# Four mixed layers on one core: six more tiles turned by way of DRAM, sums in another order, weight pieces bunched

## The chip, the cores and the metric

The kernel runs on one core of a Trainium2 chip. The metric is device time in microseconds (us) of one execution, as the median of several runs; before the change it is 1407.29 us (3 runs, 1407.14 to 1407.45). The core has five engines with a queue of instructions each: TensorE (PE in the profile, with PEld for its weight loads), VectorE (DVE), ScalarE (ACT), GpSimd (POOL) and SyncE (SP), which in this kernel issues all DMAs.

## The reference

Two kinds of layer take turns, A, B, A, B, each added to `x` (2048 rows of 512, float32), with the same weights in both rounds. Cut to what matters:

```python
def _A_ref(x, wqkv, wo):
    B, S, D = x.shape
    H = 32; Dh = D // H
    qkv = (lambda x, *d: x.transpose(*d))((x @ wqkv).reshape(B, S, 3, H, Dh), 2, 0, 3, 1, 4)
    q, k, v = qkv[0], qkv[1], qkv[2]
    phi = lambda t: jnp.where(t > 0, t + 1, jnp.exp(t)) + 1e-6
    pq, pk = phi(q), phi(k)
    kv = jnp.einsum("bhsd,bhse->bhde", pk, v)
    z = jnp.einsum("bhsd->bhd", pk)
    num = jnp.einsum("bhqd,bhde->bhqe", pq, kv)
    den = jnp.einsum("bhqd,bhd->bhq", pq, z)[..., None] + 1e-6
    o = num / den
    return (lambda x, *d: x.transpose(*d))(o, 0, 2, 1, 3).reshape(B, S, D) @ wo

def _B_ref(x, w_in, w_sp, b_sp, w_out):
    z = _gelu(jnp.einsum("bsd,df->bsf", x, w_in))
    z1 = z[..., :Fh]
    z2 = _layernorm(z[..., Fh:], axis=-1)
    g = jnp.einsum("ts,bsf->btf", w_sp, z2) + b_sp[None, :, None]
    return jnp.einsum("bsf,fd->bsd", z1 * g, w_out)

x = x + _A_ref(_layernorm(x, axis=-1), A_wqkv, A_wo)
x = x + _B_ref(_layernorm(x, axis=-1), B_w_in, B_w_sp, B_b_sp, B_w_out)
```

and the last two lines once more.

## The kernel before

The rows are cut into 16 tiles of 128 (`NT`). Every product is done as three matmuls (`mm3`, L133 to L135): each operand is split into a high half, a copy to fp32r on ACT (`high`, L119), and a low half, what is left, on DVE (`low`, L122); high by high, high by low and low by high are added up in PSUM. The order of instructions is written out by hand (`manual_schedule`): each engine runs its queue in the order in which the program names them, and waits where an operand or a buffer isn't ready.

`P1` is the first half of layer kind A, run once for each of the two rounds (`L` is 0 or 1; the text calls them first and second layer). `P1.run` has 17 steps `s`. In a step the kernel loads the rows of tile s+3, takes the statistics of tile s+2 on DVE (`ln_a`, L196 and L198) with three small operations on POOL (L200 to L203), normalises that tile on ACT (`ln_b`, L209), turns tile s (`T_high`, `T_low`), multiplies tile s-1 with the k weight (`K`) and, up to step 10, with the q weight (`Q`), applies phi to both (`phi`: L327 and L328 on ACT, L329 on DVE), splits the normalised rows (`xsplit`) and phi of k (`K_split`: L340 on ACT, L341 on DVE) and adds phi of k to the running sum on POOL (L346). `Gmm` then multiplies tile s-2's rows with its phi of k into four PSUM banks. So PE has 36 matmuls of 128x512 in a step with Q, 24 in one without. The q products of the last six tiles (`DEFER`, `later`) are done one by one afterwards, in `transition` and the first steps of `P2` (`late`, `late_phi`).

A tile is turned in one of two ways (`Turn`). By PE: the normalised tile is kept, four transposes of 128x128 go to a bank (L221), and ACT and DVE split it from there. By DRAM: ACT writes the normalised rows in another order of features, SP stores them to `xt` (L245), loads them back a step later (L249 by way of L115), and one DVE instruction (L260) turns blocks of 32x32 into a page, from which ACT and DVE split. `P1` turns tiles 10 to 15 by PE in both layers, and in the first layer tiles 0 to 2 as well; the others go by DRAM.

Beside its tiles, a step of `P1.run` also splits one piece of the weights that come next (`side`: 4 pieces of v, 4 of the output weight, 7 of `win2`; `Weight.piece` is one ACT and one DVE instruction, `fetch` one DMA). And in the first layer POOL makes sums of blocks of `w_sp` for the products of `P4`, two adds a tick (`Sums.tick`, L788), with the sums of the tick before stored to DRAM and three or one new blocks loaded; 32 ticks in all, in steps 2 to 7 of `P1`, from step 8 of `P2`, and in `P4`. In `P1` these blocks lie in two of the four large buffers `bg`.

`transition` leads from `P1` to `P2` (the rest of layer kind A and the input product of B). The first tiles of `P2` are prepared there: `a` multiplies on POOL (L567), `a2_den` takes sums and reciprocals on DVE (L579 to L581), `a2_mul` scales on DVE (L588) and copies on ACT (L240). Steps 1 to 4 of `P2.run` turn tile s by PE: `c` is the product of tile s-1, `c2` adds it to `x` (L620) and takes the statistics, `b_low` makes the low half of tile s (L122). `P4` does the product with `w_sp` and the gating; while its last loop runs over the 16 output tiles, `join` starts the next `P1`: loads, tiles 0 and 1, and the k and q weights, fetched at i = 8 and 10 and split one piece of each at i = 10 to 13.

SBUF is dealt out in slots by hand (22 pages of 128x512, 6 `qd`, 4 `bg`, and 8 PSUM banks), each list first in, first out; an instruction that fills a slot waits for the last reader of what was in it.

Of the kernel before, what the change touches and what calls it, by code (L numbers as in the profile page):

```python
# [13 lines left out]
OP = mybir.AluOpType  # L14
# [5 lines left out]
NT = S // P  # L20
# [6 lines left out]
DEFER = 6  # L27
# [44 lines left out]
def mixer_kernel(ctx: ExitStack, tc: tile.TileContext, x_in, wqkv, wo_d, win1_d, win2_d, wsp_d, bsp_d, wout_d,  # L72
                 ident_d, mask_d, out_d):
    nc = tc.nc
# [7 lines left out]
    pages = Slots(main, "pg", 22)  # L82
    quads = Slots(main, "qd", 6)
    bigs = Slots(main, "bg", 4)
# [180 lines left out]
    class P1:  # L265
        def __init__(self, L):
            self.L = L
            self.st = 2 * L
            self.x, self.ms, self.xT, self.pk, self.kb, self.r, self.xhl = {}, {}, {}, {}, {}, {}, {}
            self.wk, self.wq, self.wv = (w_square(wqkv, 512), w_square(wqkv, 0, True), w_square(wqkv, 1024))  # L270
            self.wo, self.win2 = w_wo(), w_in2()
            self.later = deque(range(NT - DEFER, NT))
            self.turn = Turn(f"xt{L}", (*((0, 1, 2) if L == 0 else ()), *range(NT - DEFER, NT)))
            self.G = None
            self.zacc = None

# [60 lines left out]
        def K_split(self, i):  # L337
            r = self.r.pop(i)
            h, l = pages.get(PAGE, F32R), pages.get(PAGE, F32R)
            nc.scalar.activation(h, r, AF.Copy, bias=PHI_EPS)  # L340
            nc.vector.scalar_tensor_tensor(l, r, PHI_EPS, h.bitcast(F32), op0=OP.add, op1=OP.subtract)  # L341
            self.pk[i] = (h, l)
            if i == 0:
                self.zacc = r
            else:
                nc.gpsimd.tensor_tensor(self.zacc, self.zacc, r, op=OP.add)  # L346
                pages.put(r)

        def Q(self, i):
            self.qb = self.proj(i, self.wq)  # L350
# [78 lines left out]
        def run(self, sums):  # L429
            side = deque()  # L430
            for w in (self.wv, self.wo, self.win2):
                side.extend([w] * len(w.pieces))
            side[0].fetch()
            ND = NT - DEFER
            for s in range(1, NT + 2):
                self.loadx(s + 3)
                self.turn.load(s + 1)
                if 2 <= s < NT:
                    self.T_high(s)
                if s == 1:  # L440
                    if not self.kb:
                        self.K(0)
                    self.K(1)
                elif 2 < s <= NT:
                    self.K(s - 1)
                self.ln_a(s + 2)
                if 2 <= s < NT:
                    self.T_low(s)
                if s <= NT:
                    self.K_phi(s - 1)  # L450
                if s <= ND:
                    self.Q(s - 1)
                if s == NT + 1:
                    self.late()
                if s <= NT:
                    self.xsplit(s - 1)
                    self.K_split(s - 1)
                self.ln_b(s + 2)
                if s <= ND:
                    self.Q_phi(s - 1)  # L460
                if s >= 2:
                    self.Gmm(s - 2)
                if s == NT + 1:
                    self.late_phi()
                if self.L == 0 and s == 2:
                    sums.slots = Sheets(bigs, 2)
                if self.L == 0 and 2 <= s < 8:
                    sums.tick(s < 7)
                if self.L == 0 and s == 8:
                    sums.store()  # L470
                    sums.slots.close()
                    sums.slots = pages
                if side:
                    side.popleft().piece()
                if side:
                    side[0].fetch()
            while side:
                side.popleft().piece()


    def transition(p1, p2):
# [9 lines left out]
        for c in range(4):  # L491
# [15 lines left out]
                                op=OP.add)  # L507
# [4 lines left out]
        for q in range(4):  # L512
            b = banks.get([P, P])
            s = slice(q * P, (q + 1) * P)
# [26 lines left out]
        p2.a2_mul(1)  # L541
        p1.late()
        p2.a(3)
        p2.a2(2)
        p1.late_phi()


    class P2:
# [69 lines left out]
        def c2(self, i):  # L618
            x = self.x[i]
            nc.vector.tensor_add(x, x, self.cb)  # L620
            banks.put(self.cb)
            self.ms[i] = stats(x, 1)

        def c3(self, i):
            x = self.x.pop(i)
# [75 lines left out]
        def run(self, sums):  # L701
            w1 = self.win1
            for s in range(1, NT + 3):
                self.loadx(s + 1)
                self.qturn.load(s + 1)
                if s in self.qturn.by_pe:
                    self.c(s - 1)
                    self.b_high(s)
                    self.c2(s - 1)
                    self.b_low(s)  # L710
                    if s >= 2:
                        self.d_high(s - 2)
                        self.d_low(s - 2)
                    self.p1.late()
                    self.c3(s - 1)
                    self.a2(s + 2)
                    self.p1.late_phi()
                    self.a(s + 3)
                else:
                    if s < NT:  # L720
                        self.b_high(s)
                    self.a2_den(s + 2)
                    if s < NT:
                        self.b_low(s)
                    if s <= NT:
                        self.c(s - 1)
                        self.c2(s - 1)
                    if s == NT:
                        quads.put(*self.W2)
                        pages.put(self.zbc)  # L730
                    self.a2_mul(s + 2)
                    late = s - 2 in self.xturn.by_pe
                    if late:
                        self.d_high(s - 2)
                        self.d_low(s - 2)
                    if s <= NT:
                        self.c3(s - 1)
                    self.a(s + 3)
                    if s <= NT + 1 and not late:
                        self.d_high(s - 2)  # L740
                        self.d_low(s - 2)
                if s >= 4:
                    self.e4(s - 4)
                self.xturn.load(s - 1)
                if s >= 3:
                    self.e(s - 3)
                    self.e2(s - 3)
                    self.e3(s - 3)
                self.f()
                self.f()  # L750
                self.fq.extend(self.fnext)
                self.fnext = []
                w1.piece(True)
                w1.fetch()
                if s > 7:
                    sums.tick()
                if s >= NT + 1:
                    self.p4.fetch(s - NT - 1)
            self.e4(NT - 1)
            self.win2.free()  # L760
# [51 lines left out]
    class P4:  # L812
# [243 lines left out]
        def join(self, i, nxt):  # L1056
# [9 lines left out]
            if i in (11, 12):  # L1066
                nxt.turn.load(i - 11)
            if 10 <= i < 14:
                nxt.wk.piece()
                nxt.wq.piece()  # L1070
            if i == 14:
                nxt.T(0)
            if i == 15:
# [2 lines left out]
    sums = Sums()  # L1076
    p1 = P1(0)
    p1.start()
    for L in range(2):
        p1.run(sums)  # L1080
        p2 = P2(p1)
# [39 lines left out]
```

## Time and profile before

| | before |
|---|---|
| median of 3 runs | 1407.29 us |
| the profiled execution, its time | 1407.07 us |
| its span, first to last instruction | 1405.3 us |
| granted TensorE clock | 1.00 |
| PE busy | 1394.3 us, 99% |
| DVE busy | 889.5 us, 63% |
| ACT busy | 572.7 us, 41% |
| POOL busy | 405.8 us, 29% |
| DMA | 219.39 MB, mean 156 GB/s |

A row of a timeline has the start in us from the span's beginning, the duration, engine, line, operation, out<-in by the program's names and shapes; in brackets stands how long the engine was idle before and what ended that. A row of the view of waits reads: who waited, for whom, us in total, how often, the longest. The first layer's `P1` runs to about 132 us in the span, the second's from about 707 to 827.

### The profile page before, as it was taken

To read this page: it belongs to the slowest core of one execution; us is meant where nothing else is said; L and a number is where in the kernel's file an instruction comes from. 1 tells how busy PE (TensorE), PEld (TensorE's weight loads), DVE (VectorE), ACT (ScalarE), POOL (GpSimd) and SP (SyncE) were. 2 spreads that over 40 slices of the span, in tenths; PEclk is the share of its full clock that TensorE was granted. 3 is DMA by queue.
4 is the path that set the end of the run, shared out by engine and by line. 5 is a ranking of instruction groups with operands and counts; after the bars stand their busy time and mean duration, and the time that the engine had idled before them with its cause. 6 is when DMAs were issued, how large, how long until landed. Compare 5 with 4: busy or idle time off the path is not lost.

```text
span 1405.3 us, 17490 instructions
## 1 busy us (share of the span) xinstructions
PE 1394.3 (99%) x6318; PEld 1167.0 (83%) x6318; DVE 889.5 (63%) x1263; ACT 572.7 (41%) x871; POOL 405.8 (29%) x490
## 2 busy tenths in 40 slices
PE   9999999999999999999999999999999999999998
PEld 7788888888888888888888888888888888888887
DVE  7876786753587666583578767766415466666632
ACT  5665544434322332351366655444333233333420
POOL 3843244544366002040023334432100030022300
PEclk9999999999999999999999999999999999999999
DMA  5831156766887433443644212555335344434432
GB/s 198 258 117 46 56 177 213 258 226 204 326 299 265 133 121 136 167 163 120 210 127 142 61 38 93 183 177 163 114 119 158 105 165 134 130 120 169 152 112 90
DMA packets 134390, 219.39 MB, mean 156 GB/s; under 512 B 11552, under 2 KB 44064, under 8 KB 134304
## 3 DMA queue, kind: packets, MB, share of 16 engines
q1 hardware_dynamic: 134304, 218.28, 47.5%
q8 instruction: 49, 0.80, 0.2%
q14 instruction: 37, 0.30, 0.1%
HBM read 153.49 MB, written 64.75 MB: 155 GB/s over the span
## 4 chain that ended last, share of the span: by engine, by line
PE 93%; DVE 2%; ACT 1%; DMA 1%; POOL 1%; issue 1%; SPq 0%; ACTq 0%; DVEq 0%; POOLq 0%
PE bank L135 18%; PE bank L134 18%; PE bank L133 18%; PE bank L908 13%; PE bank L910 13%; PE bank L909 13%; PE bank L221 1%; DMA pg<-in_wqkv_dram 1%; DVE qd L122 0%; DMA pg<-in_x_dram 0%; DVE st L196 0%; DVE pg L588 0%; ACT z_q L328 0%; ACT pg L209 0%; ACT z_q L327 0%
## 5 line engine op out<-in xcount | busy, mean ns | idle before, releaser
L908 PE MATMUL bank<-qd,pg 128*128 128x512 f32 x800 | 311.3, 389 | 0.0
L910 PE MATMUL bank<-qd,pg 128*128 128x512 f32 x800 | 311.2, 389 | 0.0
L909 PE MATMUL bank<-qd,pg 128*128 128x512 f32 x800 | 311.2, 389 | 0.0
L847 DVE TENSOR_TENSOR qd<-qd,qd 128x1024 fp32r<-128x1024 f32 x112 | 151.9, 1356 | 175.6 <-ACT qd L846 175.4
L846 ACT ACTIVATE qd<-qd 128x1024 fp32r<-128x1024 f32 x112 | 118.5, 1058 | 215.8 <-PE bank L910 195.5
L935 POOL TENSOR_TENSOR bg<-bg,pg 128x512 f32<-128x512 f32 x56 | 85.5, 1562 | 408.8 <-DVE bg L962 195.5
L910 PEld LDWEIGHTS bank<-qd,pg 128*128 128x128 f32 x800 | 150.2, 188 | 31.3
L908 PEld LDWEIGHTS bank<-qd,pg 128*128 128x128 f32 x800 | 150.1, 188 | 31.3 <-DVE bg L953 0.2
L909 PEld LDWEIGHTS bank<-qd,pg 128*128 128x128 f32 x800 | 150.2, 188 | 31.2
L135 PE MATMUL bank<-qd,pg 128*128 128x512 f32 x384 | 150.7, 392 | 3.0 <-DVE pg L122 3.0
L200 POOL TENSOR_SCALAR rs<-mv 128x1 f32<-128x1 f32 x96 | 33.1, 344 | 378.8 <-DVE mv L198 378.3
L209 ACT ACTIVATE pg<-pg,nb,rs 128x512 f32<-128x512 f32 x63 | 51.0, 810 | 181.2 <-POOL nb L203 181.2
L133 PE MATMUL bank<-qd,pg 128*128 128x512 f32 x288 | 112.7, 391 | 1.4 <-ACT pg L119 1.4
L134 PE MATMUL bank<-qd,pg 128*128 128x512 f32 x288 | 112.3, 390 | 0.0
L133 PE MATMUL bank<-bg,qd 128*128 128x448 f32 x256 | 94.0, 367 | 0.0
L134 PE MATMUL bank<-bg,qd 128*128 128x448 f32 x256 | 93.6, 366 | 0.0
L135 PE MATMUL bank<-bg,qd 128*128 128x448 f32 x256 | 93.4, 365 | 0.0
L788 POOL TENSOR_TENSOR pg<-pg,pg 128x512 f32<-128x512 f32 x52 | 78.0, 1499 | 47.3 <-DMA pg<-in_wsp_dram 33.8
L135 PEld LDWEIGHTS bank<-qd,pg 128*128 128x128 f32 x384 | 72.1, 188 | 21.2 <-DVE pg L122 6.4
L135 PE MATMUL bank<-qd,bg 128*128 128x512 f32 x224 | 87.5, 390 | 0.0
L135 PE MATMUL bank<-wo,qd 128*128 128x512 f32 x224 | 87.3, 390 | 0.2 <-DVE qd L122 0.2
L134 PE MATMUL bank<-qd,bg 128*128 128x512 f32 x224 | 87.4, 390 | 0.0
(128 smaller groups left out, 2640.2 us busy)
## 6 DMA issues: line engine op xcount, KB each, us to landing
qd<-s SPq DMA_DIRECT2D x64, 512.0 KB, 3.3
qd<-in_wsp_dram SPq DMA_DIRECT2D x48, 512.0 KB, 4.0
pg<-x SPq DMA_DIRECT2D x64, 256.0 KB, 3.0
z<-pg SPq DMA_DIRECT2D x56, 256.0 KB, 2.3
pg<-z SPq DMA_DIRECT2D x56, 256.0 KB, 5.3
pg<-in_wsp_dram SPq DMA_DIRECT2D x52, 256.0 KB, 4.8
s<-pg SPq DMA_DIRECT2D x52, 256.0 KB, 4.5
x<-pg SPq DMA_DIRECT2D x48, 256.0 KB, 2.6
```

Source lines behind the costliest of these rows:

```text
L133: nc.tensor.matmul(out, ah, bh, start=start, stop=False)
L134: nc.tensor.matmul(out, ah, bl, start=False, stop=False)
L135: nc.tensor.matmul(out, al, bh, start=False, stop=stop)
L200: nc.gpsimd.tensor_scalar(rs, mv[:, 1:2], LN_EPS, None, op0=OP.add)
L209: nc.scalar.activation(y, x, AF.Identity, bias=nb, scale=rs)
L788: nc.gpsimd.tensor_tensor(t, a, b, op=OP.add)
L846: nc.scalar.activation(w[:, 0], r, AF.Copy)
L847: nc.vector.tensor_sub(w[:, 1], r, w[:, 0].bitcast(F32))
L908: m(out, h[:, o], w[:, 0, j, :], start=start, stop=False, skip_group_check=True)
L909: m(out, h[:, o], w[:, 1, j, :], start=False, stop=False, skip_group_check=True)
L910: m(out, l[:, o], w[:, 0, j, :], start=False, stop=stop, skip_group_check=True)
L935: nc.gpsimd.tensor_tensor(u, u, z1, op=OP.mult)
```

## The change

Six things are changed.

1. `P1` turns all tiles by DRAM but tiles 0 to 2 of the first layer. Tile 2 of that layer is turned at the end of step 1, no longer in step 2.
2. The running sum of phi of k is written to the page of the new summand, and the page of the old sum is given back; before it was added in place.
3. The first blocks of `w_sp` are fetched in step 1. The ticks of `P1` are in steps 2 to 5, behind the statistics and before `K_split`, no longer at the end of steps 2 to 7; those of `P2` start at step 6 instead of 8.
4. The weight pieces of `side` are split one a step up to step 5 and two a step in steps 6 to 10, and none after; they are fetched one or two ahead.
5. In the steps 1 to 4 of `P2` the statistics of tile s-1 come behind `b_low`; in `transition` the second half of `a2(2)` comes behind `late_phi`.
6. In `join` both k pieces come at i = 10 and 11 and both q pieces at i = 12 and 13.

```diff
@@ -270,7 +270,7 @@
             self.later = deque(range(NT - DEFER, NT))
-            self.turn = Turn(f"xt{L}", (*((0, 1, 2) if L == 0 else ()), *range(NT - DEFER, NT)))
+            self.turn = Turn(f"xt{L}", range(3) if L == 0 else ())
@@ -343,8 +343,9 @@
             else:
-                nc.gpsimd.tensor_tensor(self.zacc, self.zacc, r, op=OP.add)
-                pages.put(r)
+                nc.gpsimd.tensor_tensor(r, self.zacc, r, op=OP.add)
+                pages.put(self.zacc)
+                self.zacc = r
@@ -435,7 +436,8 @@
                 self.turn.load(s + 1)
-                if 2 <= s < NT:
+                turned = 2 <= s < NT and s not in self.turn.by_pe
+                if turned:
                     self.T_high(s)
@@ -444,7 +446,12 @@
                 self.ln_a(s + 2)
-                if 2 <= s < NT:
+                if self.L == 0 and s == 1:
+                    sums.slots = Sheets(bigs, 2)
+                    sums.fetch()
+                if self.L == 0 and 2 <= s < 6:
+                    sums.tick(s < 5)
+                if turned:
                     self.T_low(s)
@@ -455,6 +462,8 @@
                     self.K_split(s - 1)
+                if s + 1 < NT and s + 1 in self.turn.by_pe:
+                    self.T(s + 1)
                 self.ln_b(s + 2)
@@ -462,20 +471,14 @@
-                if self.L == 0 and s == 2:
-                    sums.slots = Sheets(bigs, 2)
-                if self.L == 0 and 2 <= s < 8:
-                    sums.tick(s < 7)
-                if self.L == 0 and s == 8:
+                if self.L == 0 and s == 6:
                     sums.store()
                     sums.slots.close()
                     sums.slots = pages
-                if side:
+                for _ in range(min(len(side), 1 if s < 6 else 2)):
                     side.popleft().piece()
-                if side:
-                    side[0].fetch()
-            while side:
-                side.popleft().piece()
+                for w in list(side)[:1 if s < 5 else 2]:
+                    w.fetch()
@@ -541,8 +544,9 @@
         p2.a(3)
-        p2.a2(2)
+        p2.a2_den(2)
         p1.late_phi()
+        p2.a2_mul(2)
@@ -619,7 +623,9 @@
             banks.put(self.cb)
-            self.ms[i] = stats(x, 1)
+
+        def c_stats(self, i):
+            self.ms[i] = stats(self.x[i], 1)
@@ -708,6 +714,7 @@
                     self.c2(s - 1)
                     self.b_low(s)
+                    self.c_stats(s - 1)
@@ -725,6 +732,7 @@
                         self.c2(s - 1)
+                        self.c_stats(s - 1)
@@ -752,7 +760,7 @@
-                if s > 7:
+                if s > 5:
                     sums.tick()
@@ -1066,8 +1074,8 @@
             if 10 <= i < 14:
-                nxt.wk.piece()
-                nxt.wq.piece()
+                for _ in range(2):
+                    (nxt.wk if i < 12 else nxt.wq).piece()
```

## The prediction

> **What bounds the kernel now.** I read the page first, then the view of waits for TensorE alone, then TensorE's timeline at each of these waits.
>
> ```profile
> span 1405.3 us, 17490 instructions
> PE 1394.3 (99%) x6318; PEld 1167.0 (83%) x6318; DVE 889.5 (63%) x1263; ACT 572.7 (41%) x871; POOL 405.8 (29%) x490
> ...
> PE bank L135 <- DVE pg L122: 3.0, 5, 0.7
> ...
> PE bank L133 <- ACT pg L119: 1.4, 1, 1.4
> PE bank L135 <- DVE qd L122: 0.2, 1, 0.2
> ```
>
> TensorE (PE) is busy 99% of the span, and its waits after the warm-up add up to 3.0 + 1.4 + 0.2 = 4.6 us. So time can come out in two ways only: less work for PE, or fewer of these seven waits. And it comes back in one way: an engine that feeds PE falls behind. The timeline shows where the seven are.
>
> ```profile
> 22.69 0.39 PE L133 MATMUL bank<-qd,pg 128*128 128x512 f32 x1
> 22.92 0.39 PE L134 MATMUL bank<-qd,pg 128*128 128x512 f32 x1
> 23.83 0.50 PE L135 MATMUL bank<-qd,pg 128*128 128x512 f32 x1 [0.52 <-DVE pg L122]
> ...
> 41.40 0.50 PE L133 MATMUL bank<-qd,pg 128*128 128x512 f32 x1 [1.40 <-ACT pg L119]
> ...
> 156.19 0.50 PE L135 MATMUL bank<-qd,pg 128*128 128x512 f32 x1 [0.72 <-DVE pg L122]
> 163.40 0.50 PE L135 MATMUL bank<-qd,pg 128*128 128x512 f32 x1 [0.53 <-DVE pg L122]
> ...
> 692.56 0.50 PE L135 MATMUL bank<-wo,qd 128*128 128x512 f32 x1 [0.17 <-DVE qd L122]
> ...
> 851.11 0.51 PE L135 MATMUL bank<-qd,pg 128*128 128x512 f32 x1 [0.72 <-DVE pg L122]
> 858.32 0.50 PE L135 MATMUL bank<-qd,pg 128*128 128x512 f32 x1 [0.51 <-DVE pg L122]
> ```
>
> A 128x512 matmul starts 0.23 us after the one before (22.69, 22.92). At 23.83 the distance is 0.91, which is 0.68 too much where only 0.52 is shown as idle; the next is about 0.1 late too. So I count each wait as its idle time plus 0.27 for coming up again.
>
> **Transposes off TensorE.** Steps are those of `P1.run`; a step without Q (11 to 16) has 24 matmuls.
>
> ```profile
> L221 PE MATMUL bank<-ident,pg x132: 270/272/285, 6.3 to 878.0; 128*128 128x128 f32 x132
> ...
> 113.69 0.69 DVE L329 SCALAR_TENSOR_TENSOR pg<-bank,pg 128x512 f32<-128x512 f32 x1 [1.72 <-ACT pg L328]
> 119.60 0.69 DVE L329 SCALAR_TENSOR_TENSOR pg<-bank,pg 128x512 f32<-128x512 f32 x1 [1.72 <-ACT pg L328]
> ...
> 125.04 0.69 DVE L329 SCALAR_TENSOR_TENSOR pg<-bank,pg 128x512 f32<-128x512 f32 x1 [1.56 <-ACT pg L328]
> ```
>
> L329 follows each K product. From 113.69 to 119.60 PE does 24 matmuls and the four transposes of a tile in 5.91 us; from 119.60 to 125.04 the 24 alone, in 5.44. A turned tile costs PE 0.47 us. Of the 33 tiles (132 transposes) the change takes six in each layer away: 12 x 0.47 = **5.6 us**, if the other engines keep a pace of 5.44.
>
> What is added for each such tile: a store and a load of 256 KB, and one L260 on VectorE (DVE). Whether DVE and ScalarE (ACT) keep up is read from steps of the second layer that already turn by DRAM, where PE is not yet the limit:
>
> ```profile
> 750.13 0.69 DVE L329 SCALAR_TENSOR_TENSOR pg<-bank,pg 128x512 f32<-128x512 f32 x1 [0.46 <-ACT pg L328]
> ...
> 751.52 1.60 DVE L341 SCALAR_TENSOR_TENSOR pg<-pg,pg 128x512 fp32r<-128x512 f32 x1
> ...
> 753.99 0.68 DVE L122 TENSOR_TENSOR bg<-pg,bg 128x512 fp32r<-128x512 f32 x1
> 754.58 1.08 DVE L260 STREAM_TRANSPOSE pg<-pg 128x512 f32<-128x512 f32 x1
> ...
> 757.51 0.69 DVE L329 SCALAR_TENSOR_TENSOR pg<-bank,pg 128x512 f32<-128x512 f32 x1 [0.46 <-ACT pg L328]
> ...
> 751.40 0.80 ACT L209 ACTIVATE pg<-pg,nb,rs 128x512 f32<-128x512 f32 x1
> ...
> 755.69 0.63 ACT L119 ACTIVATE pg<-pg 128x512 fp32r<-128x512 f32 x1 [1.83 <-DVE pg L260]
> ...
> 750.91 1.66 POOL L346 TENSOR_TENSOR pg<-pg,pg 128x512 f32<-128x512 f32 x1
> ...
> 19.17 0.69 DVE L341 SCALAR_TENSOR_TENSOR pg<-pg,pg 128x512 fp32r<-128x512 f32 x1
> ...
> 35.23 1.29 POOL L346 TENSOR_TENSOR pg<-pg,pg 128x512 f32<-128x512 f32 x1
> ```
>
> L341 takes 1.60 us while GpSimd's (POOL) running sum L346 runs, and 0.69 at 19.17, where no L346 runs. They get in each other's way. With the reordered sum L346 writes the page that L341 reads, so it can only start when L341 has ended. A step without Q then needs: L329 to L341, 1.39; L341, 0.69; then L260, 1.11 until ACT's L119 may copy (754.58 to 755.69); from there 1.82 to the next L329 (757.51). The sum is **5.01**, below 5.44. With L341 at 1.60 it would be 5.92 and above it: the new order of the sum is what makes room for the transposes. The weight pieces that leave steps 11 to 15 take a further 0.59 (753.99 to 754.58) off DVE there.
>
> The other way round the loop goes through DRAM:
>
> ```profile
> DMA to landing us min/median/max: 2.3/2.8/5.9
> ```
>
> That is the answer for the tensor `xt`, stores and loads together. L209 of tile s+2 ends at 752.20, 2.07 after L329; store and load take 2 x 2.8; L260 to L329 takes 2.93. That is 10.6 for two steps, against 2 x 5.44 = 10.9 of PE: it fits by a hair, and at 5.9 for the load it does not (13.7). SyncE's queue (SP) issues the load behind the store's landing; queued behind that is an x load, needed three steps later, and past step 12 nothing.
>
> VectorE: DVE Perf Modes, in the Trainium skill, section Rules for kernel authors, speaks against this part: for a 128x128 transpose it says to use TensorE where PSUM will do. By that rule the 5.6 us would not be had, and the sum below would end at 1401.7. The rows bear it out only for a TensorE with time to spare, and here it is the one engine without; the way in which it could still be right is the second rival.
>
> **Weight pieces, two a step in steps 6 to 10.**
>
> ```profile
> 765.44 0.69 DVE L329 SCALAR_TENSOR_TENSOR pg<-bank,pg 128x512 f32<-128x512 f32 x1 [1.01 <-ACT pg L328]
> ...
> 773.60 0.69 DVE L329 SCALAR_TENSOR_TENSOR pg<-bank,pg 128x512 f32<-128x512 f32 x1 [1.17 <-ACT pg L328]
> ```
>
> With one piece, DVE and ACT turn a Q step round in 757.51 - 750.13 = 7.38 us; 36 matmuls of PE pace it at 773.60 - 765.44 = 8.16. A second piece adds its 0.59 on DVE (ACT's half overlaps the transposition): 7.97, still below. Cost 0, under PE's matmuls, with a margin of only 0.19; the second DMA a step joins the SP queue ahead of the x and `xt` loads, which are needed a step later. Without that cover it is 0.59 - 0.78 in the worst order, so 0.4 us in each of 10 steps.
>
> **The start of the first layer.**
>
> ```profile
> 30.39 3.24 POOL L788 TENSOR_TENSOR bg<-bg 128x512 f32<-128x512 f32 x2 [4.11 <-DMA bg<-in_wsp_dram]
> ...
> 35.31 0.82 ACT L209 ACTIVATE pg<-pg,nb,rs 128x512 f32<-128x512 f32 x1 [2.76 <-POOL nb L203]
> ```
>
> The wait at 23.83 is for tile 2's low part (L122). Moved to the end of step 1, that stands behind the L341 at 19.17 on DVE and is there by about 20.5 (19.17 + 0.69 + 0.68), before K wants it: 0.52 + 0.27 = **0.8 us**. The wait at 41.40 begins on POOL, which stood 4.11 us for the first pieces of `wsp`, with the layer norm's small operations queued behind; ACT's L209 waited 2.76 for these. Fetched in step 1, the pieces have some 10 us more. All of it is 1.40 + 0.27 = 1.7. But the two adds of a tick now come before L346, and so beside L122 and L341 on DVE, each able to hold one up by 1.29, and tiles 3 and 4 come with little to spare. Bounds 0 and 1.7; nearer the upper, since only the one L122 before L260 lies in the loop: **1.0**. The two ticks that go to `P2`'s steps 6 and 7 have idle POOL time; the first wait for `wsp` there cost POOL 3.69 us before, in step 8, and PE nothing:
>
> ```profile
> 232.30 1.29 POOL L788 TENSOR_TENSOR pg<-pg,pg 128x512 f32<-128x512 f32 x1 [3.69 <-DMA pg<-in_wsp_dram]
> ```
>
> **Into the second half of each layer.**
>
> ```profile
> 154.65 0.69 DVE L196 BATCH_NORM_STATS2 st<-pg 128x6 f32<-128x512 f32 x1
> ...
> 155.48 0.66 DVE L122 TENSOR_TENSOR pg<-bank,pg 128x512 fp32r<-128x512 f32 x1
> ...
> 149.59 0.63 ACT L240 ACTIVATE pg<-pg 128x512 f32<-128x512 f32 x1 [1.42 <-DVE pg L588]
> 151.52 0.63 ACT L240 ACTIVATE pg<-pg 128x512 f32<-128x512 f32 x1 [1.30 <-DVE pg L588]
> 152.06 0.58 ACT L327 ACTIVATE z_q<-bank 128x512 f32<-128x512 f32 x1
> ```
>
> PE waits at 156.19 for L122 of 155.48. The statistics before it (154.65 to 155.48, 0.83) now come after. And `late_phi`'s L327 no longer stands behind the second L240: it can start at 150.1, 1.9 earlier, with the L588 of 0.69 now after it. So L122 is ready some 2 us earlier, and the wait (0.72 + 0.27) goes. The second wait, 0.53 + 0.27, would first grow, because PE now arrives 1 us sooner; against it stand the same 0.83 and what is left of the 1.2 us upstream. Bounds for a layer: 1.1 (the second stays nearly whole) and 1.8 (both go); I take 1.6, by the sizes of the two savings: **3.2 us** in two layers.
>
> **The join.**
>
> ```profile
> 689.55 0.63 ACT L119 ACTIVATE qd<-pg 128x512 fp32r<-128x512 f32 x1 [5.40 <-DMA pg<-in_wqkv_dram]
> ```
>
> ACT waited 5.40 us for a q weight issued in the same step, with the split of `P4`'s next tile queued behind it, and PE then 0.17 at 692.56. With both k pieces first, q has two more steps: 0.17 + 0.27 = **0.4 us**.
>
> **The sum.** 5.6 + 0.8 + 1.0 + 3.2 + 0.4 = 11.0 us. The profiled execution took 1407.07 (its span 1405.3 and 1.8 around it), 0.2 below the median of 1407.29: 1407.07 - 11.0 = **1396.1 us**. With the upper bounds (1.7, 3.6) it is 1395.0, with the lower (0, 2.2) 1398.1.
>
> **Rivals.**
>
> First, the adds hold up the start. If the adds cost L122 and L341 1.29 us in each of steps 3 to 5, the loop of 7.38 becomes 8.67, 0.5 over PE's 8.16: the 1.0 is lost and 1.5 more, 1398.6. For it: the L341 of 1.60. Against it: steps with adds at the end already ran without a wait of PE after 41.40.
>
> Second, turned tiles come late. At 2.8 for the store and 5.9 for the load, two steps take 13.7, so 6.85 a step, 1.41 over 5.44. Over five steps that is 7.0 a layer, less about 2 that L329 has in hand (it waits 1.72 for ACT): 10 in both layers, 1406; halfway, 1401. Against it: 5.9 was met while `wsp` was being loaded, and steps 11 to 16 load little.
>
> Third, the new sum doesn't part L341 and L346, because something else holds L346. Then steps 11 to 15 run at 5.92: 0.48 x 5 less 1.7 in hand, 0.7 a layer: 1397.5.
>
> Fourth, slower: L346, pushed back, falls on the weight subtraction. Both take two SBUF inputs, as L341 does. L346 would run from 752.21 to 753.50, and L122 starts at 753.99: 0.49 apart. If L346 starts over 0.49 late, L122 waits up to 1.29, and L122 lies in the loop. One-piece steps become 8.67 (0.51 over 8.16, in 3 + 4 steps), two-piece steps 9.26 (1.10 over, in 10): 3.6 + 11.0 = 14.6 lost, 1410.7. SBUF — State Buffer in the Trainium skill, section SBUF: two separate sides, says that of VectorE and GpSimd the one that starts first holds the shared pair of ports for its whole instruction and the other blocks; by that rule the conflict can only move, which is this rival. The trace agrees as to the price (0.69 becomes 1.60).
>
> **Chances.** Forecast 0.56, own range 1395.0 to 1398.1; adds at the start 0.17; late tiles 0.13; third rival 0.06; fourth 0.08. A measurement here can tell about 0.2%, 2.8 us, from no change: faster is below 1404.5, slower above 1410.1. The forecast, the first and third rival and most of the second are faster: 0.56 + 0.17 + 0.06 + 0.12 = 0.91. The fourth gives slower 0.05 and, partly met, 0.03 same; the worst of the second 0.01 same. The range reaches from 1394, a little below the best sum, to 1403, which takes in the first and third rival and the middle of the second; the fourth stays out.
>
> **What would show it.** L221 x84 in place of x132. L341 near 0.69, with L346 after it. L329 every 5.44 us in steps 11 to 16 and 8.16 in 6 to 10. No wait of PE near 24, 41, 153 to 163, 690 and 845 to 860. Wrong would be: PE waiting for L119 or L122 in steps 6 to 16 (second or fourth rival), or L122 of a weight at over 1 us.

## The result and the profile after

| | before | after |
|---|---|---|
| median | 1407.38 us (6 runs, 1407.14 to 1407.58) | 1402.16 us (6 runs, 1401.15 to 1403.45) |
| ratio of the times, 95% interval | | 0.9962 (0.9952 to 0.9972) |
| profiled execution, its span | 1405.3 us | 1400.1 us |

The kernel became 5.2 us faster; 11.0 were forecast. The time lies in the range of 1394 to 1403, and the sign is right, but not within the bounds of the sum, 1395.0 to 1398.1: half of the expected gain is missing. Where it went is the question of all that follows.

The head of the page of after, then its waits of TensorE, as those of before were shown (who waited, for whom, us in total, how often, the longest):

```profile
span 1400.1 us, 17475 instructions
PE 1390.0 (99%) x6270; PEld 1162.0 (83%) x6270; DVE 878.8 (63%) x1275; ACT 571.9 (41%) x871; POOL 399.9 (29%) x490
...
PE bank L133 <- ACT z_h L119: 1.4, 1, 1.4
PE bank L133 <- ACT pg L119: 1.4, 4, 0.6
PE bank L133 <- ACT qd L119: 1.0, 1, 1.0
```

The 48 transposes are gone (x6318 to x6270). All seven waits of before are gone too: no line waits for L122 any more, and the one on `pg` L119 has become four others. But 3.8 us of new waits stand there, six of them. TensorE's timeline places them:

```profile
30.60 0.39 PE L135 MATMUL bank<-pg,pg 128*128 128x512 f32 x1
31.60 0.50 PE L133 MATMUL bank<-qd,pg 128*128 128x512 f32 x1 [0.61 <-ACT pg L119]
31.94 0.39 PE L134 MATMUL bank<-qd,pg 128*128 128x512 f32 x1
32.33 0.50 PE L135 MATMUL bank<-qd,pg 128*128 128x512 f32 x1
32.66 0.39 PE L133 MATMUL bank<-qd,pg 128*128 128x512 f32 x1
...
58.60 0.50 PE L133 MATMUL bank<-qd,pg 128*128 128x512 f32 x1 [0.29 <-ACT pg L119]
...
98.67 0.50 PE L133 MATMUL bank<-qd,z_h 128*128 128x512 f32 x1 [1.41 <-ACT z_h L119]
...
216.49 0.47 PE L133 MATMUL bank<-bg,qd 128*128 128x448 f32 x1 [1.04 <-ACT qd L119]
```

Matmuls of this shape start 0.23 apart. After 30.60 the four distances are 1.00, 0.34, 0.39 and 0.33: 1.14 too long together where 0.61 is idle. So a wait ahead of a whole product costs its idle time plus 0.53 (two halves come late, L133's and then L135's; the low half, an L122, ends at 32.27 on DVE), not plus 0.27 as I had taken from the wait at 23.83. By the distances the four waits from 31.60 to 58.60, 9.0 apart, cost 3.5 (1.4 and four times 0.53), the one at 98.67 2.0 and the one at 216.49 1.6; 0.33 more is lost at 241.07, in the same loop.

One mark divides the time: the transposes in `transition` just before TensorE turns to the second half of a layer. In the first layer they start at

```profile
144.40 0.60 PE L221 MATMUL bank<-ident,pg 128*128 128x128 f32 x4
```

before, and after at

```profile
144.51 0.60 PE L221 MATMUL bank<-ident,pg 128*128 128x128 f32 x4
```

so the whole first half of the first layer gained nothing, where 4.6 were forecast (2.8 of transposes, 0.8 and 1.0 at the start). In the second layer the same mark stands at 839.32 and 836.35 (each with the matmul from which it is counted, before and then after). Counted from the same matmul of that layer's second K product, at 709.87 and 709.75, 129.45 becomes 126.60. That is 2.85, and six times 0.47 is 2.82.

```profile
709.87 0.50 PE L135 MATMUL bank<-qd,pg 128*128 128x512 f32 x1
...
839.32 0.60 PE L221 MATMUL bank<-ident,pg 128*128 128x128 f32 x4
```

```profile
709.75 0.50 PE L135 MATMUL bank<-qd,pg 128*128 128x512 f32 x1
...
836.35 0.60 PE L221 MATMUL bank<-ident,pg 128*128 128x128 f32 x4
```

The books after: second layer 2.85, the four waits into the second halves 3.6 (the distances between the matmuls at these places), the join 0.4, first layer's first half -0.1, first layer's second half -1.95 (1.62 + 0.33): 4.8 of the 5.2 on the span. The last matmul starts at 1400.76 before and at 1395.93 after, 4.83 earlier; the other 0.4 lies behind it, in the end of the program, and its cause is open. One profile's books are good to some 0.3: `p2_prefetch`, below, runs the same program up to the first layer's mark, has that mark at 144.25 and shows no wait near 31.6, its first being at 40.37.

What holds TensorE at 31.60 to 58.60 is seen on VectorE (DVE) and GpSimd (POOL), here for step 3. L796 are the two adds of a tick (L788 before):

```profile
32.73 0.69 DVE L329 SCALAR_TENSOR_TENSOR pg<-bank,pg 128x512 f32<-128x512 f32 x1 [0.46 <-ACT pg L328]
33.34 1.84 DVE L122 TENSOR_TENSOR pg<-pg,pg 128x512 fp32r<-128x512 f32 x1
35.11 1.78 DVE L341 SCALAR_TENSOR_TENSOR pg<-pg,pg 128x512 fp32r<-128x512 f32 x1
36.81 0.68 DVE L329 SCALAR_TENSOR_TENSOR z_q<-bank,z_q 128x512 f32<-128x512 f32 x1
37.41 1.45 DVE L122 TENSOR_TENSOR qd<-pg,qd 128x512 fp32r<-128x512 f32 x1
38.78 1.07 DVE L260 STREAM_TRANSPOSE pg<-pg 128x512 f32<-128x512 f32 x1
...
41.70 0.69 DVE L329 SCALAR_TENSOR_TENSOR pg<-bank,pg 128x512 f32<-128x512 f32 x1 [0.46 <-ACT pg L328]
```

```profile
33.33 3.01 POOL L796 TENSOR_TENSOR bg<-bg 128x512 f32<-128x512 f32 x2
37.02 1.29 POOL L346 TENSOR_TENSOR pg<-pg,pg 128x512 f32<-128x512 f32 x1 [0.68 <-issue]
```

Three instructions of 0.69 take 1.84, 1.78 and 1.45. The first two each stand beside one of the adds. L346 must wait for the L341 so delayed, begins at 37.02, and falls on the subtraction of the weight piece. L260 stands behind all three in DVE's order. So the loop is 41.70 - 32.73 = 8.97, not 8.16, and 0.81 is lost in each of these steps. The section SBUF: two separate sides of SBUF — State Buffer in the Trainium skill says that the one of VectorE and GpSimd that starts first holds the shared ports for its whole instruction; the trace agrees in that L122 and L341 are late by 1.15 and 1.09, near the 1.29 of one POOL instruction alone, and the piece by 0.76, where 0.90 of L346 was left.

### The profile page after: what moved, and what is told of

The parts are those of the page before. It is cut to its first block, busy times and chain, and to the rows that moved or that the text cites. A ratio compares the mean times of both kernels' runs of the same rounds, so it can differ in the third digit from the quotient of the medians.

```text
span 1400.1 us, 17475 instructions
## 1 busy us (share of the span) xinstructions
PE 1390.0 (99%) x6270; PEld 1162.0 (83%) x6270; DVE 878.8 (63%) x1275; ACT 571.9 (41%) x871; POOL 399.9 (29%) x490
## 4 chain that ended last, share of the span: by engine, by line
PE 83%; DMA 1%; DVE 0%; ACT 0%; SPq 0%; issue 0%; POOL 0%; POOLq 0%
PE bank L135 15%; PE bank L134 15%; PE bank L133 15%; PE bank L917 13%; PE bank L916 13%; PE bank L918 13%; DMA pg<-in_x_dram 1%; PE bank L221 0%; SPq L115 0%; DVE qd L122 0%; ACT qd L119 0%; DVE st L196 0%; ACT z_z L209 0%; SPq L791 0%; DVE pg L1011 0%
## 5 line engine op out<-in xcount | busy, mean ns | idle before, releaser
L916 PEld LDWEIGHTS bank<-qd,pg 128*128 128x128 f32 x800 | 150.1, 188 | 31.6
L918 PEld LDWEIGHTS bank<-qd,pg 128*128 128x128 f32 x800 | 150.2, 188 | 31.1
L917 PEld LDWEIGHTS bank<-qd,pg 128*128 128x128 f32 x800 | 150.1, 188 | 30.9
L135 PE MATMUL bank<-qd,pg 128*128 128x512 f32 x384 | 150.4, 392 | 0.1
L200 POOL TENSOR_SCALAR rs<-mv 128x1 f32<-128x1 f32 x96 | 37.4, 390 | 374.0 <-DVE mv L198 370.5
L209 ACT ACTIVATE pg<-pg,nb,rs 128x512 f32<-128x512 f32 x63 | 51.1, 810 | 181.8 <-POOL nb L203 181.7
L133 PE MATMUL bank<-qd,pg 128*128 128x512 f32 x288 | 112.8, 392 | 1.4 <-ACT pg L119 1.4
L796 POOL TENSOR_TENSOR pg<-pg,pg 128x512 f32<-128x512 f32 x56 | 82.2, 1468 | 48.4 <-DMA pg<-in_wsp_dram 42.1
L133 PE MATMUL bank<-bg,qd 128*128 128x448 f32 x256 | 94.2, 368 | 1.0 <-ACT qd L119 1.0
L135 PE MATMUL bank<-bg,qd 128*128 128x448 f32 x256 | 93.7, 366 | 0.1
L135 PE MATMUL bank<-qd,bg 128*128 128x512 f32 x224 | 87.5, 390 | 0.0
L134 PE MATMUL bank<-qd,bg 128*128 128x512 f32 x224 | 87.4, 390 | 0.0
L133 PE MATMUL bank<-qd,bg 128*128 128x512 f32 x224 | 87.2, 389 | 0.0
L133 PE MATMUL bank<-wo,qd 128*128 128x512 f32 x224 | 87.1, 389 | 0.0
```

The costliest lines, as they stand in the source:

```text
L133: nc.tensor.matmul(out, ah, bh, start=start, stop=False)
L134: nc.tensor.matmul(out, ah, bl, start=False, stop=False)
L135: nc.tensor.matmul(out, al, bh, start=False, stop=stop)
L200: nc.gpsimd.tensor_scalar(rs, mv[:, 1:2], LN_EPS, None, op0=OP.add)
L209: nc.scalar.activation(y, x, AF.Identity, bias=nb, scale=rs)
L796: nc.gpsimd.tensor_tensor(t, a, b, op=OP.add)
```

## The experiments

For the wait at 98.67, the wait of step 10 from here on, there were two theories. A: step 10 itself takes 7.98 us on DVE and ACT (two pieces), the step after it has only the 5.44 of 24 matmuls on TensorE, and the difference has to come from a lead, the time by which the engines that feed TensorE are ahead of it, built up earlier; the adds of steps 2 to 5 have used that lead up. B: the wait is made at its own place, whatever went before (the first of the tiles newly turned by DRAM come late). DVE's rows there, of after:

```profile
91.82 0.69 DVE L329 SCALAR_TENSOR_TENSOR pg<-bank,pg 128x512 f32<-128x512 f32 x1 [0.46 <-ACT pg L328]
...
95.67 1.28 DVE L122 TENSOR_TENSOR bg<-pg,bg 128x512 fp32r<-128x512 f32 x2
96.87 1.07 DVE L260 STREAM_TRANSPOSE pg<-pg 128x512 f32<-128x512 f32 x1
...
99.80 0.69 DVE L329 SCALAR_TENSOR_TENSOR pg<-bank,pg 128x512 f32<-128x512 f32 x1 [0.39 <-ACT pg L328]
101.19 0.69 DVE L341 SCALAR_TENSOR_TENSOR pg<-pg,pg 128x512 fp32r<-128x512 f32 x1
...
104.81 0.69 DVE L329 SCALAR_TENSOR_TENSOR pg<-bank,pg 128x512 f32<-128x512 f32 x1 [0.53 <-ACT pg L328]
```

99.80 - 91.82 is 7.98, and 104.81 - 99.80 is 5.01. L260 has no wait for a DMA ahead of it there, it runs on behind the two pieces.

**The ticks back at the end of the step** (`sums_end`), with the early fetch kept:

```diff
-                if self.L == 0 and 2 <= s < 6:
-                    sums.tick(s < 5)
                 if turned:
@@
                     self.late_phi()
+                if self.L == 0 and 2 <= s < 6:
+                    sums.tick(s < 5)
```

> The changed kernel, but the ticks of steps 2 to 5 of the first layer's first half stand at the end of the step again (behind Q_phi and Gmm); the early fetch in step 1 stays. Theory A (the two adds ahead of K_split hold L122 and L341 on VectorE, make the step 9.0 us instead of 8.16, and leave no slack for step 11): L341 falls from about 1.8 to 0.7 in these steps, the waits of TensorE at 31.6, 40.6, 49.6 and 58.6 (3.6 us with the restarts) shrink below 1.5 us in all, and the wait near 98.7 (2.0 us) shrinks to under 1 or goes; about 1398 to 1400 us. Theory B (the wait near 98.7 is the round trip of a turned tile through DRAM): that wait stays at 1.4 us or more, since no DMA of tiles 10 to 15 is changed; about 1399 to 1401 us.

Measured: 1398.30 us, 0.9939 (0.9925 to 0.9954), span 1395.8. DVE at the same step:

```profile
31.34 0.69 DVE L329 SCALAR_TENSOR_TENSOR pg<-bank,pg 128x512 f32<-128x512 f32 x1 [0.46 <-ACT pg L328]
...
32.74 0.69 DVE L341 SCALAR_TENSOR_TENSOR pg<-pg,pg 128x512 fp32r<-128x512 f32 x1
...
35.19 1.47 DVE L122 TENSOR_TENSOR qd<-pg,qd 128x512 fp32r<-128x512 f32 x1
...
39.52 0.69 DVE L329 SCALAR_TENSOR_TENSOR pg<-bank,pg 128x512 f32<-128x512 f32 x1 [0.45 <-ACT pg L328]
```

The collisions of L341 and of the first L122 are gone (L122 takes 0.68 at 31.95). One is left: the piece now meets the adds themselves, which stand on POOL from 34.82 for 3.00. The loop is 8.18, and no wait is left before 94. The mark of the first layer moves from 144.51 to 140.71. The wait of step 10 stays, with 0.96 idle instead of 1.41: just under the 1 that A allowed, and not the 1.4 of B, but too near to decide, since a loop of 8.18 against 8.16 builds no lead either. That the place of the adds made the start slow is shown; A against B is not.

**The first blocks of `wsp` for the second half fetched a step earlier** (`p2_prefetch`):

```diff
                     sums.tick()
+                elif s == 5 and self.L == 0:
+                    sums.fetch()
```

> The changed kernel with one fetch of the blocks of w_sp in step 5 of P2, ahead of the first tick there in step 6. Theory A (GpSimd stands for the landing of these blocks, with the layer norm's small operations behind it): the adds start at about 207 instead of 211, the wait of TensorE at 216.5 (1.6 us with the restart) goes, about 1400.3 us. Rival: it is the two adds themselves, 2.6 us, or the four loads ahead of the x and qt loads: the wait stays above 0.8 us and the time within 0.8 us of 1402.2.

In after, the first tick of `P2` stands thus on POOL and ACT:

```profile
211.08 2.65 POOL L796 TENSOR_TENSOR pg<-pg,pg 128x512 f32<-128x512 f32 x2 [4.00 <-DMA pg<-in_wsp_dram]
```

```profile
215.10 0.81 ACT L209 ACTIVATE pg<-pg,nb,rs 128x512 f32<-128x512 f32 x1 [8.92 <-POOL nb L203]
```

POOL stands 4.00 for the blocks, the small operations of the layer norm (L203 the last) stand behind the adds, ACT waits 8.92 for them, and TensorE 1.04 for ACT's split behind this L209. With the fetch a step earlier the adds run at 206.72:

```profile
206.72 2.99 POOL L798 TENSOR_TENSOR pg<-pg,pg 128x512 f32<-128x512 f32 x2
```

and the wait at 216 is gone. 1400.06 us, 0.9950 (0.9934 to 0.9967): 2.1 less than after, 1.95 by the books.

**One piece in step 10, the last in step 11** (`piece_11`):

```diff
-                for _ in range(min(len(side), 1 if s < 6 else 2)):
+                for _ in range(min(len(side), 1 if s < 6 or s > 9 else 2)):
                     side.popleft().piece()
-                for w in list(side)[:1 if s < 5 else 2]:
+                for w in list(side)[:1 if s < 5 or s > 8 else 2]:
```

> The changed kernel, but step 10 splits one weight piece and step 11 the last one (two a step in steps 6 to 9 alone). Theory A (step 10 of VectorE and ScalarE takes 7.97 us while TensorE has only 5.44 us between K of tile 10 and K of tile 11): the wait near 98.7 falls by 0.6, from 1.41 idle to about 0.8; about 1401.5 us. Theory B (round trip through DRAM): the wait stays at 1.4.

Measured: 1402.46 us, 0.9967 (0.9956 to 0.9978), no difference from after. The wait of step 10 shrinks by 0.6, one piece on DVE; but a new one comes a step later, and one L122 of step 11 shows why:

```profile
98.09 0.50 PE L133 MATMUL bank<-qd,z_h 128*128 128x512 f32 x1 [0.80 <-ACT z_h L119]
...
104.95 0.50 PE L133 MATMUL bank<-qd,z_h 128*128 128x512 f32 x1 [0.78 <-ACT z_h L119]
```

```profile
101.84 1.39 DVE L122 TENSOR_TENSOR bg<-pg,bg 128x512 fp32r<-128x512 f32 x1 [0.53 <-ACT bg L119]
```

```profile
101.39 1.29 POOL L346 TENSOR_TENSOR pg<-pg,pg 128x512 f32<-128x512 f32 x1 [1.46 <-DVE pg L341]
```

On POOL L346 runs from 101.39 to 102.68, across the start of the piece, which takes 1.39 instead of 0.68. In step 10 of after two pieces lie behind L329 without such a meeting (1.28 for both). That it was DVE's work in step 10 that was late, as A says, this shows; and also that a step without Q has no room for a piece, which is what the change's "none after step 10" bought.

**Tiles 10 to 15 by TensorE again** (`turn_by_pe`), all else as after:

```diff
-            self.turn = Turn(f"xt{L}", range(3) if L == 0 else ())
+            self.turn = Turn(f"xt{L}", (*((0, 1, 2) if L == 0 else ()), *range(NT - DEFER, NT)))
@@
-                turned = 2 <= s < NT and s not in self.turn.by_pe
+                turned = 2 <= s < NT and (s > 2 or self.L)
@@
-                if s + 1 < NT and s + 1 in self.turn.by_pe:
+                if s == 1 and self.L == 0:
```

> The changed kernel, but tiles 10 to 15 are turned by TensorE again in both layers, at their old place in the step. If the price of 0.47 us a tile holds, the second layer grows by 2.8 us; in the first the same 2.8, less what is left of the 2.0 us near 98.7, which should go to the most part because the transposes give VectorE and ScalarE time: 1405 to 1406 us. If turning by DRAM were worth nothing, 1402 us.

Measured: 1405.02 us, 0.9984 (0.9975 to 0.9993): 2.9 more than after, not 5.6. The waits of TensorE:

```profile
PE bank L133 <- ACT pg L119: 1.0, 4, 0.3
```

The wait of step 10 is gone (TensorE now has the transposes to do there), and so, nearly, is the one at 216, for which TensorE now comes later. What the turning by DRAM is worth is thus 2.8 in the second layer, as forecast (129.43 from 710.08 to 839.51, against the 126.60 of after). In the first it is little as long as the start is late: from the last of the four waits to the mark it is 0.75 (86.66 against 85.91), and the second layer's K products come only 0.33 later than in after.

**No adds in the first half of the first layer** (`p1_no_adds`), their ticks put behind, two a step in steps 9 to 14 of `P2`, is the clean test of A against B:

```diff
-                if self.L == 0 and s == 1:
-                    sums.slots = Sheets(bigs, 2)
-                    sums.fetch()
-                if self.L == 0 and 2 <= s < 6:
-                    sums.tick(s < 5)
@@
-                if s > 5:
-                    sums.tick()
+                if s > 7:
+                    for _ in range(2 if 9 <= s < 15 else 1):
+                        sums.tick()
```

> The changed kernel without any tick in the first layer's first half: no adds and no blocks of w_sp there. P2 ticks once in step 8, twice in steps 9 to 14 and once after, so that as many are done before P4 as before. Theory A (adds in steps 2 to 5 hold VectorE, so that there is no slack when step 10 of 7.97 us meets the 5.44 us of step 11): the step is 7.4 us until TensorE paces it, the waits at 31.6 to 58.6 (3.6 us) and near 98.7 (2.0 us) are all gone, and that at 216.5 (1.6 us) too, as the first tick is in step 8 again; 1394.5 to 1396 us, unless the double ticks cost something. Theory B (the wait near 98.7 is the round trip of a turned tile through DRAM): that wait stays at 0.9 us idle or more.

No instruction of TensorE waits between 20 and 234 us: not in steps 2 to 5, and not in step 10 either, which has its two pieces and its newly turned tiles as in after. The mark of the first layer:

```profile
139.64 0.60 PE L221 MATMUL bank<-ident,pg 128*128 128x128 f32 x4
```

4.87 earlier than after. A holds and B falls: with the adds away the early steps build up the lead that step 10 uses. The total is nevertheless worse, 1413.66 us, 1.0047 (1.003 to 1.0063): in the second half POOL now stands for the blocks, and TensorE behind it, 9.8 us in four waits.

```profile
244.38 2.66 POOL L788 TENSOR_TENSOR pg<-pg,pg 128x512 f32<-128x512 f32 x2 [3.73 <-DMA pg<-in_wsp_dram]
```

```profile
PE bank L133 <- ACT qd L119: 9.8, 4, 3.3
```

**The same with the blocks fetched a step ahead** (`no_adds_prefetch`: as the last, and `sums.fetch()` in step 7 of `P2`).

> As the kernel without adds in the first half, and one fetch of blocks of w_sp in step 7 of P2 ahead of the first tick in step 8. Theory A: in step 8 there is room, so that it changes nothing on TensorE: within 0.5 us of that kernel. If GpSimd's wait for the first blocks still reaches TensorE there: 0.5 to 2 us faster.

1409.82 us, 1.0018 (1.0009 to 1.0028), with 8.2 us in four waits left instead of 9.8. The fetch ahead gives 3.8 back and not the whole, more than either expectation had. The two profiled executions are only 1.2 apart (1412.60 and 1411.41), so they don't show where all of the 3.8 comes from, and which of the doubled ticks makes each wait stays open. The adds can be moved, but not all to this place.

**The running sum in place again** (`sum_in_place`):

```diff
-                nc.gpsimd.tensor_tensor(r, self.zacc, r, op=OP.add)
-                pages.put(self.zacc)
-                self.zacc = r
+                nc.gpsimd.tensor_tensor(self.zacc, self.zacc, r, op=OP.add)
+                pages.put(r)
```

> The changed kernel, but the running sum of phi of k is in place again, so that L346 may start together with L341. If the new order is what parts the two: L341 is 1.5 to 1.6 us again, a step without Q needs 5.9 us where TensorE has 5.44, TensorE waits some 0.4 us in each of steps 12 to 15 of the first layer (no slack there) and little in the second (some 3 us of slack); 1403 to 1405 us. If the order doesn't matter: 1402 us and L341 at 0.7.

```profile
100.27 1.60 DVE L341 SCALAR_TENSOR_TENSOR pg<-pg,pg 128x512 fp32r<-128x512 f32 x1
```

```profile
PE bank L134 <- DVE pg L341: 1.3, 5, 0.6
```

1405.86 us, 0.9986 (0.9977 to 0.9996): 3.7 more than after. L341 is back at 1.60 in the steps from 11 on and TensorE waits for it; four of the five waits lie in the first layer. The loss is 2.4 by the second layer's K products and 1.2 from there to that layer's mark, where TensorE has a single listed wait, of 0.2: late starts too short to be listed add up too. In steps 3 to 5, on the other hand, the loop is 8.7 and not 8.97: L346 no longer waits for the late L341. No wait of TensorE is listed there, but the products that waited at 31.60 and 40.57 start 8.70 apart, so about 0.5 a step is still lost. The new order of the sum is right where no adds run, and the worse one beside adds.

**The statistics ahead of the low part again** (`stats_first`, `a2(2)` whole before `late_phi` too):

```diff
-        p2.a2_den(2)
+        p2.a2(2)
         p1.late_phi()
-        p2.a2_mul(2)
@@
-                    self.b_low(s)
                     self.c_stats(s - 1)
+                    self.b_low(s)
```

> The changed kernel, but in steps 1 to 4 of P2 the statistics stand ahead of b_low again, and in the transition a2(2) is whole ahead of late_phi. The four waits of TensorE of the kernel before, 0.72 and 0.53 idle in each layer, come back near 155, 161, 847 and 854: 3.4 us with the restarts, about 1405.5 us. If these waits went for another reason (TensorE's arrival, the missing transposes): 1402 to 1403 us.

```profile
PE bank L135 <- DVE pg L122: 2.6, 4, 0.7
PE bank L133 <- ACT qd L119: 0.5, 1, 0.5
```

1404.85 us, 0.998 (0.9971 to 0.9989). The four waits come back with 2.6 idle, 3.6 with their restarts by the books; TensorE then arrives later at the first tick of `P2` and waits 0.5 there, not 1.0. Net 2.7 more than after. The two parts of this edit were not taken apart, so what each is worth alone is not shown.

**Both repairs together** (`end_prefetch`: ticks at the end of the step, as in `sums_end`, and the fetch of `p2_prefetch`).

> Both repairs at once: the ticks of steps 2 to 5 at the end of the step, and a fetch of blocks in step 5 of P2. Theory A: the two gains are at different places and add up: no wait of TensorE at 31 to 59 and near 212; what stays is the wait near 95 (1.0 idle, 1.6 with the restart), since steps of 8.2 us build no slack; about 1396.5 us.

1396.76 us, 0.9925 (0.9912 to 0.9939). Besides the warm-up, one wait is left, that of step 10:

```profile
95.03 0.50 PE L133 MATMUL bank<-qd,z_h 128*128 128x512 f32 x1 [0.97 <-ACT z_h L119]
```

**Fewer adds at the start** (`two_ticks`): as the last, with ticks in steps 2 and 3 alone, and two a step in the steps 16 and 17 of `P2`, where no more tiles are prepared:

```diff
-                if self.L == 0 and 2 <= s < 6:
-                    sums.tick(s < 5)
@@
+                if self.L == 0 and 2 <= s < 4:
+                    sums.tick(s < 3)
-                if self.L == 0 and s == 6:
+                if self.L == 0 and s == 4:
@@
-                    sums.tick()
+                    for _ in range(2 if s in (16, 17) else 1):
+                        sums.tick()
+                elif s == 5 and self.L == 0:
+                    sums.fetch()
```

> As the kernel with both repairs, but the first half has ticks in steps 2 and 3 alone, and P2 ticks twice in steps 16 and 17 instead, behind its last loads. Theory A: steps 4 and 5 take 7.4 us on VectorE and ScalarE where TensorE needs 8.16, which gives 1.6 us of slack; with the 0.16 of each of steps 6 to 10 that covers the wait near 95: it goes. TensorE has no wait left between 20 and 130 us; about 1395 us, if the double ticks in steps 16 and 17 hold nothing up. If they do (as in steps 9 to 14 of the kernel without adds): a wait near 310 to 330 us, up to 2.5 us each.

1395.38 us, 0.9915 (0.9901 to 0.9928), four runs within 0.25: the lowest median of all, 6.8 below after. In its view of waits TensorE waits nowhere behind the warm-up. The mark of the first layer is at 139.49, 4.9 before the 144.40 of the kernel before, where 4.6 were forecast. DVE's rows at step 10:

```profile
86.55 0.69 DVE L329 SCALAR_TENSOR_TENSOR pg<-bank,pg 128x512 f32<-128x512 f32 x1 [0.46 <-ACT pg L328]
...
94.53 0.69 DVE L329 SCALAR_TENSOR_TENSOR pg<-bank,pg 128x512 f32<-128x512 f32 x1 [0.39 <-ACT pg L328]
```

The step takes 7.98 here too, to the hundredth, and TensorE does not wait: with two steps free of adds ahead of it there is a lead to pay from.

**Two pieces from step 5 to 9, one in step 10** (`two_ticks_piece5`), otherwise as the last:

```diff
-                for _ in range(min(len(side), 1 if s < 6 else 2)):
+                for _ in range(min(len(side), 1 if s < 5 or s > 9 else 2)):
                     side.popleft().piece()
-                for w in list(side)[:1 if s < 5 else 2]:
+                for w in list(side)[:1 if s < 4 or s > 8 else 2]:
```

> As the kernel with ticks in steps 2 and 3 alone, and the weight pieces two a step in steps 5 to 9, one in step 10. Step 5 becomes 7.97 instead of 7.4 us, step 10 7.4 instead of 7.97: the slack in front of step 11 is the same or 0.6 more. Within 0.5 us of the kernel with two ticks if that one has no wait left near 95; otherwise up to 0.6 us faster.

1395.70 us, 0.9916 (0.9903 to 0.993): no difference. A lighter step 10 brings nothing more once the lead is there.

## Why the prediction came out at twice the gain

**Transposes, 5.6.** The price, 0.47 a tile, was right, and so was the loop without Q: 5.01 forecast, 5.01 measured from 99.80 to 104.81. The second layer gave its 2.8. (That the measured 1402.2 lies near the 1401.7 that the working gave for a change without these 5.6 is chance: what is missing is missing at other places.) In the first layer 2.0 of the 2.8 went to the wait at 98.67. The step of the working that failed here is that of the weight pieces: "7.97, still below" with its "Cost 0" was applied to all of steps 6 to 10. (The 0.4 us a step that it names without the cover doesn't follow from the 0.59 and 0.78 beside it; the sum doesn't use it.) The loop itself was right (7.97 forecast, 7.98 measured), but step 10 with its 7.98 is followed by 5.44 of TensorE's work, not by 8.16. The 2.5 between them are paid from a lead of the feeders. I counted a lead only as what L329 has in hand in late steps before the change, and did not ask what it would be at step 10 once the start was slower. `p1_no_adds` and `two_ticks` show it: the same step, no wait.

**The start of the first layer, +1.8.** It became a loss of 0.8. The wait at 23.83 went, and so did the one at 41.40; with that the early fetch did what was said of it. But the term for the adds had bounds of 0 and 1.7, and the value was -1.6: four waits that cost 3.5 in place of the one of 1.40, which with its late halves had been 1.9. That "only the one L122 before L260 lies in the loop" is the step that failed here. DVE works in order, so whatever holds L341 also holds L329 of q, the piece and L260 behind it. The first rival named this loss and gave it about 0.5 a step (8.67 against 8.16); 0.81 was measured, because the mechanism of the fourth rival came on top: L346, pushed back by the late L341, fell on the piece. Two rivals that I had set side by side happen together in the steps with adds. In after's steps without adds neither does: L341 takes 0.69 at 101.19.

**The ticks of `P2`, 0.** 1.95 was measured. The forecast took from step 8 of before that POOL may wait for the blocks (3.69) without TensorE noticing, and used that for step 6. The fetch and the tick that needs it moved together, to where TensorE has less in hand. `p2_prefetch` gave 2.1 back.

**Transitions, 3.2 and join, 0.4.** 3.6 and 0.4. All four waits went; `stats_first` brings them back. Here the step had nothing wrong in it.

**Rivals.** Late tiles (the second) were not what TensorE waited for: near 98, where it did wait, L260 ran on without a wait for its DMA. In after DVE waits 2.6 us in three for turned tiles, and no TensorE wait follows from these. The third did not either, and `sum_in_place` shows its price as 3.7, not 1.4, or 0.7 a layer: 1.2 in the second, and 2.4 net in the first, where little is in hand. The fourth as a whole, in every step with a piece, did not come: two pieces took 1.28 at 95.67.

Put together, 11.0 less 2.0 (the pieces' step 10), 2.6 (the start, from +1.8 to -0.8) and 1.95 (the ticks), with 0.4 more from the transitions, is 4.85; TensorE's last matmul came 4.83 earlier.

So the mechanisms of the gain were there in full; with the adds and the fetch placed otherwise, `two_ticks` ends at 1395.4, within a microsecond of the 1396.1 forecast for this change. What was missing in the forecast is the lead that one step hands to the next, the adds' hold on everything behind them, and the wait for blocks at its new place.

## What to carry to other kernels

A loop that takes less than the pace of the bounding engine proves that a step costs nothing only if the next step's pace is as long; where steps of unequal length follow each other, add up what each wins or loses against the bounding engine from the beginning, and see whether the account goes below nothing. An operation moved ahead in an in-order queue is priced by everything behind it, and if two engines hold each other up, as VectorE and GpSimd do here, parting one pair of instructions can push the conflict on to the next. Work that was hidden in one step takes its waits along when it moves: ask again at the new place what covers them, and fetch its data a step before.

## What the runs showed of the hardware

After a wait of TensorE of 2.36 us its granted clock was lower. In `p1_no_adds` the matmuls of 128x448 behind the wait start 0.37 apart, and 0.20 apart again from 253.57 on:

```profile
249.80 0.58 PE L133 MATMUL bank<-bg,qd 128*128 128x448 f32 x1 [2.36 <-ACT qd L119]
250.18 0.57 PE L134 MATMUL bank<-bg,qd 128*128 128x448 f32 x1
```

In the windows of the same kernel (length in us, then busy time of TensorE, its weight loads, DVE, ACT and POOL with counts, granted clock, share of the DMA engines, GB/s):

```profile
249.80:253.50 3.70, 3.70 (x10) 3.00 (x11) 2.90 (x6) 2.80 (x5) 0.62 (x2) 0.54 0.42 97
```

The granted clock is 0.54 for 3.7 us, so this wait cost some 1.7 us beyond itself (ten matmuls 0.17 late). After a wait of 1.63 at 326.37 in the same run the matmuls were back at 0.20 from the fourth distance on. Yet in `no_adds_prefetch`, at much the same place, a wait of 1.49 was followed by the slow pace, a microsecond later:

```profile
322.79 0.47 PE L133 MATMUL bank<-bg,qd 128*128 128x448 f32 x1 [1.49 <-ACT qd L119]
```

with matmuls 0.37 apart from 324.18 to 327.17. So the length of the wait alone doesn't decide; what else does is not shown. TensorE: Matmul & The Clock Gate in the Trainium skill, section Why this matters for your kernels, warns of gaps over about 3 us; here the slow pace followed waits of 2.36 and 1.49. The wait of 1.41 in after paid only its restart.
